# The loads of x of the first three units, issued by ScalarE's queue instead of SyncE's

## The chip, the cores and the metric

The kernel runs on one core of a Trainium2 chip. The metric is the device time of one execution in microseconds; lower is better. TensorE (PE, with its weight loads PEld), VectorE (DVE), ScalarE (ACT) and GpSimd (POOL) compute. SyncE (SP) computes nothing here: it only issues DMAs. ACT can issue DMAs too. All DMAs are carried by the core's 16 DMA engines.

## The reference

Two layers follow each other: a gated linear recurrence over time, and a highway feed-forward layer on its output. There are 4 sequences of 6336 steps with 256 channels, all in float32.

```python
sig = 1.0 / (1.0 + np.exp(-f_logit))
f = lower_bound + (1.0 - lower_bound) * sig
i = 1.0 - f
for t in range(S):
    h = f[:, t] * h + i[:, t] * x[:, t]
    y[:, t] = h
...
H = np.maximum(y @ w_h, 0.0)
T = 1.0 / (1.0 + np.exp(-(y @ w_t + b_t)))
out = T * H + (1.0 - T) * y
```

## The kernel before

The 25344 rows (sequences times steps) are cut into 21 units, numbered 0 to 20. A unit holds blocks of 128 rows: units 0 and 1 have 2 blocks, unit 2 has 4, units 3 to 6 have 8, the middle ones twice 8, the last ones fewer again. So a load of f_logit or of x moves 256 KiB for units 0 and 1, 512 KiB for unit 2 and 1 MiB for units 3 to 6. I call the load of f_logit of unit n "l" with its number (l0), and that of x likewise (x0).

What happens to a unit, with the letters that the kernel's table uses:

- l, x: the two loads (line 250, both through the function load, both on SP's queue)
- u: ACT takes sigmoid(-f_logit) (line 262)
- b: POOL or DVE multiplies u with x; the product is called bv (line 277)
- i, p: PE transposes u and bv so that time runs along the free axis (lines 286, 311)
- f: ACT or DVE makes the gate from the transposed u (lines 301, 299), in two halves of 128 channels
- s: DVE scans along time (line 320), again by halves of the channels; the result is y
- z, g: PE multiplies y with the weights w_t and w_h (lines 333, 145); t, d, e: ACT, DVE and POOL make the gated part (lines 356, 363, 377)
- o, c, w: PE transposes back and adds, ACT or DVE copies, SP stores (lines 393, 394, 405, 403, 411)

The order of all this is written out by hand: a long table of tokens such as `x1.0:1` (load x of unit 1, part 0, into buffer 1), which a loop at the end of the kernel turns into instructions, one after the other. `pin` keeps every instruction in that order on its engine. Tokens `k*4` are filler matmuls on zeros for PE. Each engine works in its own order, and an instruction that waits holds up all behind it.

At the start there are four things besides the units:

- `warm` (line 154): one small sigmoid on ACT, ahead of which the compiler puts ACT's table load
- `prm`: two loads of 1 KiB each, lower_bound and b_t, on ACT's queue (lines 167, 168); PE transposes them (token `pc`, line 209), and DVE makes from that the scales ncc, cc, bt and the diagonals (tokens `cc`, `dg`)
- `wt`, `wh`: the loads of the two weight matrices, 256 KiB each, on SP's queue (lines 202, 205)
- `WT`, `WH`: DVE scales the weights with cc (lines 224 and 230, 232); WT stands between the gates and the first scan's second half of unit 0, WH behind that scan

Waits for loads go by eight counters (DMAHW0 to DMAHW7 in the listings below), which are dealt out to the DMAs in the order of the program, round and round. A DMA may be issued only when the one eight places before it, which has the same counter, has landed. Before the change the order is: first prm load 0, l0 1, x0 2, l1 3, second prm load 4, l2 5, wt 6, x1 7, wh 0, x2 1, l3 2, x3 3, l4 4, x4 5, l5 6.

Of the kernel before, what the change touches and what calls it, by code (L numbers as in the profile page):

```python
# [14 lines left out]
AF = mybir.ActivationFunctionType  # L15
# [4 lines left out]
def kernel(  # L20
# [22 lines left out]
    units, at = [], 0  # L43
# [3 lines left out]
    assert at == B * S  # L47

    order = """
l0.0:0 u0.0:0 pc:0 k*4:1 x0.0:0 b0.0.0v:0 p0.0.0:1 i0.0.1:2 cc dg f0.1v:0 p0.0.1:0 i0.0.0:3 l1.0:1 u1.0:1 l2.0:2  # L50
u2.0:2 s0.1:0 f0.0v:0 i1.0.1:4 i1.0.0:5 k*16:6 wt WT f1.0:1 i2.0.0:0 s0.0:1 z0.0.1:1 x1.0:1 b1.0.0:1 p1.0.1:2 p1.0.0:3
wh WH z0.0.0:5 k*4:6 f1.1:2 i2.0.1:4 g0.0.1:6 f2.0:3 x2.0:2 t0.0.0:0 s1.1:2 g0.0.0:0 l3.0:3 s1.0:3 g1.0.1:2 z1.0.1:3
g1.0.0:5 z1.0.0:7 t0.0.1 B2.0:2 p2.0.1:1 f2.1:0 x3.0:3 p2.0.0:4 d0.0.1:0 e0.0.1 d0.0.0 d1.0.0:1 d1.0.1 k*4:0 u3.0:3
k*4:0 t1.0.1:1 e0.0.0 i3.0.1:0 i3.0.0:2 t1.0.0 e1.0.0 l4.0:4 f3.1:2 s2.1:4 s2.0:5 B3.0v:0 f3.0:1 k*4:1 e1.0.1 x4.0:4
g2.0.0:1 d2.0.0:2 z2.0.0:0 t2.0.0:2 g2.0.1:3 k*1:2 o0.0.0:2 p3.0.1:0 l5.0:0 u4.0:0 z2.0.1:4 t2.0.1 e2.0.0 x5.0:0
# [95 lines left out]

    warm = sb([P, 64], FP32, "warm")
    nc.gpsimd.memset(warm, 0.0)
    nc.scalar.activation(warm, warm, AF.Sigmoid)
# [12 lines left out]
    nc.scalar.dma_start(prm[:NH], lower_bound.rearrange("(h p) -> h p", p=P))
    nc.scalar.dma_start(prm[NH:], moe_b_t.rearrange("(h p) -> h p", p=P))
# [74 lines left out]
    def rows(full, at, j0, j1):  # L243
        return full[at + j0 * P:at + j1 * P, :].rearrange("(p j) d -> p j d", p=P)

    def load(n, s, name, src, slot):
        at, subs = units[n]
        t = sb([P, NB, D], FP32, name, slot)
        j0 = sum(subs[:s])
        pin(nc.sync.dma_start(t[:, :subs[s]], rows(src, at, j0, j0 + subs[s])))  # L250
# [201 lines left out]
```

## Time and profile before

| what | value |
|---|---|
| median of 3 runs | 208.8 us (208.2 to 209.44) |
| the profiled execution's own time | 208.83 us |
| its span, first to last instruction | 207.1 us |
| mean granted TensorE clock | 1.000 |
| moved by the DMA engines | 78.67 MB, 380 GB/s on average |
| reads, writes of HBM | 52.43 MB, 25.95 MB |

The profile comes from one execution. A row of its timeline gives the start in us from the span's start, the time it took in us, the engine, the line of the kernel, the operation, out<-in, the shapes and the count of merged instructions; in brackets stands the idle time of the engine before it and what ended that. ACTq and SPq are the parts of ACT and SP that issue DMAs. The busy shares count instructions that compute; the slices cut the span into 40 equal stretches of 5.2 us. In the page's list of DMA queues, q1 is SP's and q10 is ACT's.

### The profile page before, as it was taken

The page shows a single profiled execution, that of the slowest core. Times are in us where ns is not written, and L with a number is a line of the kernel's source. Part 1 is how long each engine was busy: PE and PEld are TensorE (multiplying, and loading weights), DVE is VectorE, ACT ScalarE, POOL GpSimd, SP SyncE. Part 2 cuts the span into 40 slices and gives each one's busy share as a digit, 9 for nine tenths or more (in the row PEclk, how much of TensorE's full clock was granted, in tenths as well). Part 3 has the DMA queues.
Part 4 walks back from the last instruction along what each step waited for, and adds up shares of the span by engine and source line. Part 5 has one row for each costly group of instructions (what it writes and reads, how often), then busy time and mean ns, then how long its engine had stood idle before and what let it go on. Part 6 is the DMA issues. An engine that isn't in the chain of part 4 may idle for free.

```text
span 207.1 us, 4606 instructions
## 1 busy us (share of the span) xinstructions
PE 194.7 (94%) x1850; PEld 135.0 (65%) x1850; DVE 192.8 (93%) x141; ACT 190.9 (92%) x173; POOL 171.9 (83%) x90
## 2 busy tenths in 40 slices
PE   7999988998799999999989999999999999999991
PEld 2566657556566858747846967658767587677780
DVE  2799989999999999999999979999999999999971
ACT  4479699999999999999998999999999999998792
POOL 3173798978999999978998899979979949999920
PEclk9999999999999999999999999999999999999999
DMA  6999999999999999999999999999999999934576
GB/s 178 365 425 416 418 423 418 418 419 412 425 418 420 420 419 421 424 417 419 427 415 418 423 414 429 418 417 427 412 424 390 403 325 352 364 141 161 206 304 253
DMA packets 15980, 78.67 MB, mean 380 GB/s; under 512 B 1748, under 2 KB 2264, under 8 KB 10072
## 3 DMA queue, kind: packets, MB, share of 16 engines
q1 hardware_dynamic: 15952, 78.39, 93.5%
q8 instruction: 14, 0.23, 0.5%
q14 instruction: 6, 0.05, 0.1%
q10 hardware_dynamic: 8, 0.00, 0.0%
HBM read 52.43 MB, written 25.95 MB: 379 GB/s over the span
## 4 chain that ended last, share of the span: by engine, by line
PE 48%; DVE 17%; ACT 16%; DMA 11%; issue 4%; POOL 2%; SPq 1%; DVEq 0%; ACTq 0%
PE psum L333 13%; PE psum L145 11%; DMA l<-in_f_logit_dram 11%; DVE y L320 10%; PE psum L393 6%; DVE d L363 6%; PE psum L394 6%; ACT f L301 6%; PE psum L286 6%; PE psum L311 5%; ACT u L262 4%; ACT t L356 3%; ACT o L405 2%; POOL bv L277 2%; DVE f L299 1%
## 5 line engine op out<-in xcount | busy, mean ns | idle before, releaser
L277 POOL TENSOR_TENSOR bv<-u,x 128x1024 bf16<-128x1024 f16 (+2 forms) x44 | 99.8, 2293 | 18.3 <-ACT f L301 7.4
L320 DVE TENSOR_TENSOR_SCAN y<-f,y,psum 128x1024 bf16<-128x1024 f16 (+6 forms) x40 | 103.7, 2614 | 1.0 <-ACT f L301 0.6
L377 POOL TENSOR_TENSOR d<-d,t 128x1024 bf16<-128x1024 bf16 (+3 forms) x35 | 71.7, 2063 | 11.4 <-ACT t L356 6.1
L333 PE MATMUL psum<-y,w_sb 128*128 128x512 bf16 (+1 forms) x224 | 77.4, 367 | 3.0 <-ACT f L301 1.9
L145 PE MATMUL psum<-y,w_sb 128*128 128x512 bf16 x184 | 69.7, 379 | 0.7 <-DVE y L320 0.7
L363 DVE SCALAR_TENSOR_TENSOR d<-y,ncc,psum 128x1024 bf16<-128x1024 bf16 (+2 forms) x56 | 62.6, 1147 | 3.4 <-PE psum L145 1.5
L356 ACT ACTIVATE t<-psum,bt 128x1024 bf16<-128x1024 f32 (+2 forms) x56 | 56.3, 1038 | 2.6 <-PE psum L145 1.7
L262 ACT ACTIVATE u<-l 128x2048 f16<-128x2048 f32 (+2 forms) x28 | 48.6, 1747 | 5.4 <-DMA l<-in_f_logit_dram 5.4
L301 ACT ACTIVATE f<-psum,ncc 128x1024 f16<-128x1024 f16 (+3 forms) x38 | 50.9, 1365 | 1.6 <-PE psum L286 1.6
L405 ACT COPY o<-psum 128x1024 f32<-128x1024 f32 (+1 forms) x49 | 48.5, 1031 | 2.2 <-PE psum L394 1.0
L393 PE MATMUL psum<-diag,y 128*128 128x128 f16 x396 | 48.8, 219 | 0.6 <-ACT f L301 0.4
L394 PE MATMUL psum<-ident_b,d 128*128 128x128 bf16 x396 | 48.6, 219 | 0.8 <-DVE d L377 0.8
L394 PEld LDWEIGHTS <-d 128*128 128x128 bf16 x396 | 44.0, 113 | 4.8 <-DVE d L377 1.2
L393 PEld LDWEIGHTS <-y 128*128 128x128 bf16 x396 | 44.2, 113 | 2.5
L333 PEld LDWEIGHTS <-w_sb 128*128 128x128 f16 x224 | 21.6, 98 | 18.1 <-issue 1.0
L145 PEld LDWEIGHTS <-w_sb 128*128 128x128 f16 x184 | 17.9, 97 | 21.3 <-issue 6.0
L311 PE MATMUL psum<-ident_f,bv 128*128 128x128 f32 x198 | 29.3, 276 | 1.3 <-POOL bv L277 0.8
L286 PE MATMUL psum<-ident_h,u 128*128 128x128 f16 x396 | 28.6, 219 | 1.2 <-ACT u L262 0.8
L286 PEld LDWEIGHTS <-u 128*128 128x128 f16 x396 | 25.0, 98 | 6.9 <-ACT u L262 2.1
L311 PEld LDWEIGHTS psum<-ident_f,bv 128*128 128x128 f32 x198 | 22.4, 141 | 7.1 <-POOL bv L277 2.1
L377 DVE TENSOR_TENSOR d<-d,t 128x1024 bf16<-128x1024 bf16 (+3 forms) x15 | 10.6, 718 | 0.2
L145 PE MATMUL psum<-zeros 128*128 128x512 bf16 x39 | 10.6, 399 | 0.0
(33 smaller groups left out, 38.6 us busy)
## 6 DMA issues: line engine op xcount, KB each, us to landing
out_dram<-o SPq DMA_DIRECT2D x48, 512.0 KB, 7.9
l<-in_f_logit_dram SPq DMA_DIRECT2D x23, 1024.0 KB, 14.6
x<-in_x_dram SPq DMA_DIRECT2D x23, 1024.0 KB, 14.4
l<-in_f_logit_dram SPq DMA_DIRECT2D x2, 512.0 KB, 5.9
x<-in_x_dram SPq DMA_DIRECT2D x2, 512.0 KB, 7.4
l<-in_f_logit_dram SPq DMA_DIRECT2D x3, 256.0 KB, 3.7
x<-in_x_dram SPq DMA_DIRECT2D x3, 256.0 KB, 5.5
out_dram<-o SPq DMA_DIRECT2D x3, 256.0 KB, 5.6
```

The costliest lines, as they stand in the source:

```text
L145: return pe.add_instruction(mybir.InstMatmult(name=nc.get_next_instruction_name(), start_tensor_calc=start, stop_tensor_calc=stop, tile_si ...
L277: shared(pin(e.tensor_mul(st[n]["bv", s][:, a:c].rearrange("p k d j -> p k j d"), st[n]["u", s][:, 2 * a:2 * c].rearrange("p (k j) d -> p ...
L286: pin(nc.tensor.transpose(uT[:, j * P:(j + 1) * P], st[n]["u", s][:, j, h * P:(h + 1) * P], ident_h))
L301: pin(nc.scalar.activation(to, of, AF.Identity, scale=ncc[:, h:h + 1], bias=1.0))
L311: pin(nc.tensor.transpose(words[:, k:k + g * (P - 1) + 1:g], pair, ident_f))
L320: pin(nc.vector.tensor_tensor_scan(y[:, c:e], st[n]["f", h][:, c:e], data, 0.0 if fresh else carry[h], op0=ALU.mult, op1=ALU.add))
L333: pin(nc.tensor.matmul(p.part(a, e), w, data, start=ki == 0, stop=ki == NH - 1))
L356: pin(nc.scalar.activation(half(n, q, "t", m), z, AF.Sigmoid, bias=bt[:, m:m + 1]))
L363: pin(nc.vector.scalar_tensor_tensor(half(n, q, "d", m), y, ncc[:, m:m + 1], g, op0=ALU.mult, op1=ALU.max))
L377: shared(pin(e.tensor_mul(d, d, t)), not eng)
L393: pin(nc.tensor.matmul(o, st[n]["y", h][:, whole], diag[:, h], start=True, stop=False))
L394: pin(nc.tensor.matmul(o, half(n, q, "d", h)[:, cols], ident_b, start=False, stop=True))
```

## The change

Three tokens, x0, x1 and x2, leave the table. In their place, ahead of the loop over the table, ACT issues these three loads, with the two prm loads behind the first, and the small sigmoid `warm` follows behind all five.

```diff
-l0.0:0 u0.0:0 pc:0 k*4:1 x0.0:0 b0.0.0v:0 p0.0.0:1 i0.0.1:2 cc dg f0.1v:0 p0.0.1:0 i0.0.0:3 l1.0:1 u1.0:1 l2.0:2
+l0.0:0 u0.0:0 pc:0 k*4:1 b0.0.0v:0 p0.0.0:1 i0.0.1:2 cc dg f0.1v:0 p0.0.1:0 i0.0.0:3 l1.0:1 u1.0:1 l2.0:2
...
-    nc.scalar.activation(warm, warm, AF.Sigmoid)
...
-    nc.scalar.dma_start(prm[:NH], lower_bound.rearrange("(h p) -> h p", p=P))
-    nc.scalar.dma_start(prm[NH:], moe_b_t.rearrange("(h p) -> h p", p=P))
...
-    def load(n, s, name, src, slot):
+    def load(n, s, name, src, slot, queue=nc.sync):
...
-        pin(nc.sync.dma_start(t[:, :subs[s]], rows(src, at, j0, j0 + subs[s])))
+        pin(queue.dma_start(t[:, :subs[s]], rows(src, at, j0, j0 + subs[s])))
...
+    ahead = "x0.0:0 x1.0:1 x2.0:2"
+    for k, token in enumerate(ahead.split()):
+        name, _, slot = token.partition(":")
+        n, s = [int(c) for c in name[1:].split(".")]
+        load(n, s, name[0], xs if name[0] == "x" else logits, slot, nc.scalar)
+        if k == 0:
+            pin(nc.scalar.dma_start(prm[:NH], lower_bound.rearrange("(h p) -> h p", p=P)))
+            pin(nc.scalar.dma_start(prm[NH:], moe_b_t.rearrange("(h p) -> h p", p=P)))
+    pin(nc.scalar.activation(warm, warm, AF.Sigmoid))
```

On SP, at the start of the program, these rows stood before the change (l_98 is l0, x_107 x0, l_126 l1, l_130 l2, x_171 x1, x_198 x2, l_206 l3; the brackets name the counters that a row waits for):

```order
L250 DMA l_98<-in_f_logit_dram 128x512
L250 DMA x_107<-in_x_dram 128x512
L250 DMA l_126<-in_f_logit_dram 128x512
L250 DMA l_130<-in_f_logit_dram 128x1024
L202 DMA w_raw_94<-in_moe_w_t_dram 128x2x256
L250 DMA x_171<-in_x_dram 128x512
L205 DMA w_raw_94<-in_moe_w_h_dram 128x2x256 [waits DMAHW0_49]
L250 DMA x_198<-in_x_dram 128x1024 [waits DMAHW1_49]
L250 DMA l_206<-in_f_logit_dram 128x2048 [waits DMAHW2_49]
```

Now SP has these rows at the same place (l_104 is l0, l_130 l1, l_134 l2, l_206 l3, x_225 x3, l_267 l4, x_284 x4, l_309 l5; the lines moved up by three):

```order
L247 DMA l_104<-in_f_logit_dram 128x512
L247 DMA l_130<-in_f_logit_dram 128x512
L247 DMA l_134<-in_f_logit_dram 128x1024
L199 DMA w_raw_91<-in_moe_w_t_dram 128x2x256 [waits DMAHW0_49]
L202 DMA w_raw_91<-in_moe_w_h_dram 128x2x256 [waits DMAHW1_49]
L247 DMA l_206<-in_f_logit_dram 128x2048 [waits DMAHW2_49]
L247 DMA x_225<-in_x_dram 128x2048 [waits DMAHW3_49]
L247 DMA l_267<-in_f_logit_dram 128x2048 [waits DMAHW4_49]
L247 DMA x_284<-in_x_dram 128x2048 [waits DMAHW5_49]
L247 DMA l_309<-in_f_logit_dram 128x2048 [waits DMAHW6_49,Activation_49]
```

The three loads of x are gone from SP, wt and wh moved up to places four and five, and the counters are dealt anew: x0 0, l0 1, first prm load 2, l1 3, second prm load 4, l2 5, x1 6, x2 7, wt 0, wh 1, l3 2. So wt now waits for x0's landing, wh for l0's and l5 for x1's.

On ACT, at the start of the program, these rows stood before (u_100, u_128 and u_132 are u of units 0, 1 and 2):

```order
L167 DMA prm_88<-in_lower_bound_dram 2x128
L154 ACT_TABLE_LOAD
L154 ACTIVATE warm_63<-warm_63 128x64 [waits Pool_49]
L168 DMA prm_88<-in_moe_b_t_dram 2x128
L262 ACTIVATE u_100<-l_98 128x512 [waits DMAHW1_49]
L262 ACTIVATE u_128<-l_126 128x512 [waits DMAHW3_49]
L262 ACTIVATE u_132<-l_130 128x1024 [waits DMAHW5_49]
```

Now ACT has these (x_95, x_99 and x_101 are x0, x1 and x2; u_106, u_132 and u_136 are u of units 0, 1 and 2):

```order
L247 DMA x_95<-in_x_dram 128x512
L416 DMA prm_87<-in_lower_bound_dram 2x128
L417 DMA prm_87<-in_moe_b_t_dram 2x128
L247 DMA x_99<-in_x_dram 128x512
L247 DMA x_101<-in_x_dram 128x1024
L418 ACT_TABLE_LOAD
L418 ACTIVATE warm_63<-warm_63 128x64 [waits Pool_49]
L259 ACTIVATE u_106<-l_104 128x512 [waits DMAHW1_49]
L259 ACTIVATE u_132<-l_130 128x512 [waits DMAHW3_49]
L259 ACTIVATE u_136<-l_134 128x1024 [waits DMAHW5_49]
```

Five DMAs stand ahead of the table load and of the first sigmoid, where one stood before. The order on PE, DVE and POOL is the same as before.

More of the change, by code (lines that the diff above doesn't have):

```diff
@@ L49 @@
     order = """
-l0.0:0 u0.0:0 pc:0 k*4:1 x0.0:0 b0.0.0v:0 p0.0.0:1 i0.0.1:2 cc dg f0.1v:0 p0.0.1:0 i0.0.0:3 l1.0:1 u1.0:1 l2.0:2
-u2.0:2 s0.1:0 f0.0v:0 i1.0.1:4 i1.0.0:5 k*16:6 wt WT f1.0:1 i2.0.0:0 s0.0:1 z0.0.1:1 x1.0:1 b1.0.0:1 p1.0.1:2 p1.0.0:3
-wh WH z0.0.0:5 k*4:6 f1.1:2 i2.0.1:4 g0.0.1:6 f2.0:3 x2.0:2 t0.0.0:0 s1.1:2 g0.0.0:0 l3.0:3 s1.0:3 g1.0.1:2 z1.0.1:3
+l0.0:0 u0.0:0 pc:0 k*4:1 b0.0.0v:0 p0.0.0:1 i0.0.1:2 cc dg f0.1v:0 p0.0.1:0 i0.0.0:3 l1.0:1 u1.0:1 l2.0:2
+u2.0:2 s0.1:0 f0.0v:0 i1.0.1:4 i1.0.0:5 k*16:6 wt WT f1.0:1 i2.0.0:0 s0.0:1 z0.0.1:1 b1.0.0:1 p1.0.1:2 p1.0.0:3
+wh WH z0.0.0:5 k*4:6 f1.1:2 i2.0.1:4 g0.0.1:6 f2.0:3 t0.0.0:0 s1.1:2 g0.0.0:0 l3.0:3 s1.0:3 g1.0.1:2 z1.0.1:3
 g1.0.0:5 z1.0.0:7 t0.0.1 B2.0:2 p2.0.1:1 f2.1:0 x3.0:3 p2.0.0:4 d0.0.1:0 e0.0.1 d0.0.0 d1.0.0:1 d1.0.1 k*4:0 u3.0:3
```

## The prediction

> **What bounds the kernel now.** I read the page first: the busy shares and the slices of the DMA.
>
> ```profile
> PE 194.7 (94%) x1850; PEld 135.0 (65%) x1850; DVE 192.8 (93%) x141; ACT 190.9 (92%) x173; POOL 171.9 (83%) x90
> GB/s 178 365 425 416 418 423 418 418 419 412 425 418 420 420 419 421 424 417 419 427 415 418 423 414 429 418 417 427 412 424 390 403 325 352 364 141 161 206 304 253
> ```
>
> PE, DVE and ACT are busy 92 to 94% each, so none of them has room for work that comes late. The DMA moves about 420 GB/s from the third slice on; its first slice (5.2 us) has 178. The chain that ended last, in order of time, has two long transfers, of 22 us together:
>
> ```profile
> 2.11 5.94 DMA l<-in_f_logit_dram
> ...
> 8.85 16.13 DMA l<-in_f_logit_dram
> ```
>
> Both are at the start: l2 until 8.05 and l5 until 25. Behind that no transfer stands among its longest pieces. The kernel is therefore bound by loads until 25 us and by three full engines behind that. Windows show how full:
>
> ```profile
> 0.00:5.00 5.00, 3.81 (x10) 1.31 (x11) 1.08 (x5) 2.17 (x3) 1.61 (x11) 1.00 0.70 178
> 5.00:10.00 5.00, 5.00 (x30) 2.57 (x29) 3.76 (x12) 2.41 (x4) 0.36 (x1) 1.00 0.93 353
> 10.00:15.00 5.00, 4.72 (x39) 3.28 (x38) 4.71 (x12) 3.24 (x5) 4.20 (x4) 1.00 1.02 424
> 40.00:60.00 20.00, 17.33 (x166) 11.95 (x165) 19.83 (x13) 19.89 (x16) 17.90 (x8) 1.00 1.01 419
> ```
>
> Behind the stretch and its length stand the busy times of PE, PEld, DVE, ACT and POOL, last the GB/s. From 40 to 60 DVE is busy 19.83 of 20 us and ACT 19.89. A delay that both still have there reaches the end. The change is all in the first 5 us, so what matters is how much of it is left at 25 to 30 us. Next I read the timeline of DVE, since it is the fullest engine there:
>
> ```profile
> 4.20 0.73 DVE L277 TENSOR_TENSOR bv<-u,x 128x512 bf16<-128x512 f16 x1 [3.06 <-ACT u L262]
> 7.65 0.48 DVE L299 TENSOR_SCALAR f<-psum,ncc 128x256 f16<-128x256 f16 x1
> 8.80 0.62 DVE L224 TENSOR_SCALAR w_sb<-w_raw,cc 128x256 f16<-128x256 f32 x2 [0.66 <-DMA w_raw<-in_moe_w_t_dram]
> 9.33 0.68 DVE L320 TENSOR_TENSOR_SCAN y<-f,psum 128x256 bf16<-128x256 f16 x1
> 10.22 0.72 DVE L230 SCALAR_TENSOR_TENSOR w_sb<-w_raw,cc,ndiag 128x128 f16<-128x128 f32 x1 [0.21 <-DMA w_raw<-in_moe_w_h_dram]
> ...
> 16.95 2.72 DVE L277 TENSOR_TENSOR bv<-u,x 128x2048 bf16<-128x2048 f16 x1
> 20.56 4.58 DVE L320 TENSOR_TENSOR_SCAN y<-f,y,psum 128x1024 bf16<-128x1024 f16 x2 [0.26 <-PE psum L311]
> 28.19 2.35 DVE L320 TENSOR_TENSOR_SCAN y<-f,y,psum 128x1024 bf16<-128x1024 f16 x1 [0.62 <-ACT f L301]
> ...
> 35.08 1.28 DVE L363 SCALAR_TENSOR_TENSOR d<-y,ncc,psum 128x1024 bf16<-128x1024 bf16 x1 [0.36 <-PE psum L145]
> ```
>
> DVE waits for the two weight matrices, 0.66 us for w_t (landed just before 8.80) and 0.21 us for w_h (10.2). From 10.22 to 28.2 it has only two idle stretches of note, 0.26 and 0.62 us. So **the two weight loads start the chain of DVE**, and whatever delays them moves it, less 0.9 us at most.
>
> **The change part by part.** *SP's queue.* Three loads leave it, so l1 and l2 are issued about 0.45 us sooner; the DMA engines still work on l0 then. w_t now waits for x0's landing, w_h for l0's. Both then are issued at some 4 us, and six loads of 2 MiB are still queued, so the DMA has work. The later loads (l5 waits for x1's counter in place of w_t's) have long cover: l5 was issued at 8.85 and moved only at about 23 to 25.
>
> *The order of the data.* This is the term that counts. In the old single queue w_t was fifth, behind l0, x0, l1 and l2. Now SP's queue has l0, l1, l2 ahead of it, and ACT's has x0, x1, x2, of the same 1 MiB. If the DMA engines take turns between the two queues, both MiB are through at the same moment, and w_t and w_h come after all six. The same eight transfers were done when these rows say:
>
> ```profile
> 9.53 0.33 SPq L250 DMA_DIRECT2D x<-in_x_dram  x1
> 10.26 0.33 SPq L250 DMA_DIRECT2D l<-in_f_logit_dram  x1
> 11.53 0.33 SPq L250 DMA_DIRECT2D x<-in_x_dram  x1
> ```
>
> Each of these issues waits for the counter of an older load: x1, w_h and x2, landed at about 9.5, 10.2 and 11.5. The bytes are the same, so I take the same total, 11.5, for all eight, and w_h is now the last: 11.5. w_t is before it by one 256 KiB share, 10.26 - 9.53 = 0.73: 10.75. So w_t lands 1.95 us later.
>
> The Trainium skill, "DMA: Bandwidth & Descriptors", section "Issuing engines are not separate DMA queues", says that loads from several engines run on the same 16 DMA engines and that a second issuer saves only issue time. By it the total stays at 11.5, as I take it; by its opposite see the second rival.
>
> *DVE.* w_t's product goes from 8.80 to 10.76. The scan behind it ran from 9.33 to 10.01, so it ends at 11.97; w_h is there at 11.5, and its products start at 11.98 instead of 10.22: **+1.76**. That holds for the product bv of unit 3 as well, because DVE's rows have no idle time between 10.22 and 19.67 (16.95 + 2.72).
>
> *From there to ACT.* PE takes bv of unit 3 from DVE and goes on in its order, through its last matmuls of unit 2, to the transposes of u4, which ACT needs:
>
> ```profile
> 22.48 0.61 PE L286 MATMUL psum<-ident_h,u 128*128 128x128 f16 x8
> 23.18 1.11 ACT L301 ACTIVATE f<-psum,ncc 128x1024 f16<-128x1024 f16 x1 [0.81 <-PE psum L286]
> 25.07 1.91 ACT L262 ACTIVATE u<-l 128x2048 f16<-128x2048 f32 x1 [0.77 <-DMA l<-in_f_logit_dram]
> ```
>
> f4 goes from 23.18 to 24.94 and ends at 26.05; l5 is there as before at 25.0 (the same 7.5 MiB, its own among them, are through by then). u5 starts at about 26.0 instead of 25.07: **+0.93**; the 0.77 us in which ACT waited for l5 are used up. f4's second half and DVE's scan at 28.19 follow ACT: 29.1. DVE's own work before that scan ended at 28.19 - 0.62 = 27.57, and now at 27.57 + 1.76 - 0.26 = 29.07. Both are late by 0.9, and both are full from there: +0.9 at the end.
>
> *ACT's queue.* Five DMA issues now stand ahead of the table load. Before:
>
> ```profile
> 0.73 0.54 ACTq L167 DMA_DIRECT2D prm<-in_lower_bound_dram  x1
> 1.18 0.42 SPq L250 DMA_DIRECT2D x<-in_x_dram  x1
> 1.31 1.28 ACT L154 ACT_TABLE_LOAD   x1 [1.31 <-PEq L436]
> 1.38 0.24 ACTq L168 DMA_DIRECT2D prm<-in_moe_b_t_dram  x1
> 2.60 0.26 ACT L154 ACTIVATE warm<-warm 128x64 f32<-128x64 f32 x1
> 3.06 0.47 SPq L250 DMA_DIRECT2D x<-in_x_dram  x1
> 3.47 0.63 ACT L262 ACTIVATE u<-l 128x512 f16<-128x512 f32 x1 [0.61 <-DMA l<-in_f_logit_dram]
> 3.86 0.26 PE L209 MATMUL psum<-ident_f,prm 4*128 4x4 f32 x1
> ```
>
> A 128-row load takes 0.42 to 0.47 us to issue on SP and is not shown on ACT. By these rows, x0 0.42, two prm 0.24 each, x1 and x2 0.47 each and five gaps of 0.05 end at 2.8; with 1.28 and 0.26 u0 starts at 4.35 instead of 3.47, +0.9. At 0.54 for each, the dearest issue on ACT, it is 5.2, +1.7. Either is hidden: f0's second half would end at 8.13 + 0.9 = 9.0, at most 9.9, and w_t is there at 10.75. If w_t came on time, only the 0.66 us of waiting would cover it.
>
> *The small loads prm.* They now stand behind x0 in ACT's queue, and PE's transpose of prm, first in PE's order but for the six warm-up matmuls, waits for both. How two busy queues share an engine is shown by one event, the data packets of the two prm loads, the only ones on ACT's queue. The first load's stand in the 0.1 us from 1.6, with its counter writes:
>
> ```profile
> q10 hardware_dynamic: 4, 0.00, 4.2%
> ```
>
> The second load's stand in the 0.1 us from 3.1:
>
> ```profile
> q10 hardware_dynamic: 2, 0.00, 3.4%
> ```
>
> The first needed 0.9 to 1.0 us from its issue at 0.73, with nothing else queued. The second was issued at 1.38, so it was ready near 2.3 and waited 0.8 us more, until about the end of l0 (u0 starts on it at 3.47). I read that as turns of a whole load's share. Then, on the two engines that carry prm, its first load follows l1 and its second follows l2:
>
> ```profile
> 5.37 0.63 ACT L262 ACTIVATE u<-l 128x512 f16<-128x512 f32 x1 [1.28 <-DMA l<-in_f_logit_dram]
> 8.08 1.06 ACT L262 ACTIVATE u<-l 128x1024 f16<-128x1024 f32 x1 [2.07 <-DMA l<-in_f_logit_dram]
> ```
>
> l1 landed before 5.37 and l2 before 8.08, on the slowest engine. l2's 512 KiB need 1.24 us at the 424 GB/s of the window from 10, so its share is through between 6.6 and 8.05. At 6.6 the transpose moves by 2.74, and with it what hangs on PE: f0's second half ends at 8.13 + 2.74 = 10.87, 0.1 behind w_t, which I leave out. At 8.1 it is the first rival; with short turns it is nothing. I take 6.6: the later end is that of one engine, the earlier the rate of most rows.
>
> *What comes sooner gains nothing.* x1 and x2 land about 3 and 1.5 us sooner, but unit 1's scans stand behind w_h's products on DVE, and unit 2's behind those.
>
> Sum: the profiled execution took 208.83 us (span 207.1 and 1.7 around it), 0.03 over the median of 208.8. 208.83 + 0.93 = **209.8**, slower by 0.45%.
>
> **The rivals.**
> 1. *prm behind a late l2.* If the engines with prm are among the late ones, prm's transpose comes at 8.1, +4.2. f0's second half ends at 12.4, w_h's products start at 13.6, +3.4, and u5 is late by 3.4 - 0.8 = 2.6: 211.4. For it: PE's row of the transpose stands ahead of all its other work but the warm-up. Against it: l2's 8.05 is the landing of the slowest engine, and the two with prm must be among those.
> 2. *The start gets faster.* In windows of 0 to 5 and 5 to 10 us the DMA moved 0.89 and 1.77 MB; at the 424 GB/s of the next window these need 6.3 us instead of the 8.3 since the first packets at about 1.7. If two queues win all of that, w_t is there at 8.8 and prm early (short turns). DVE then is late only by ACT's queue, 0.9 less the 0.66 and 0.21 of waiting, and ACT need not wait for l5: u5 starts at 24.5, -0.6, DVE at 27.7, -0.45: 208.4. At best all three early waits of DVE (0.26, 0.62 and 0.36) go: 207.7. It decides from the point where w_t lands before 9.1. For it: SP issues almost without a break at the start. Against it is the poorest stretch, 4.25 to 6.5, with over 1 MiB queued (eight loads of 2.5 MiB issued by 4.52, under 0.9 MB moved by 5.0), where more issuers add nothing (the DMA in that stretch, and SP's eighth issue):
>
> ```profile
> DMA packets 249, 0.57 MB, mean 253 GB/s; under 512 B 23, under 2 KB 109, under 8 KB 249
> ```
>
> ```profile
> 4.05 0.47 SPq L250 DMA_DIRECT2D x<-in_x_dram  x1
> ```
>
>    The Trainium skill, "Perfetto Trace Analysis", section "DMA Optimizations", says that spreading issues may help when the issuing engine's track is solid with them; it is, and this rival is what that would give.
> 3. *No effect.* SP's queue is served first while it has work: w_t keeps its time, only x comes later, and the rest hides: 208.8 to 209.0.
>
> **How the numbers follow.** The forecast has 0.52, the rivals 0.22, 0.18 and 0.08. About 0.5% is what a measurement of this kernel can tell from no change, here 1.04 us. The forecast's own range is 209.3 to 210.3 (a queue that starts sooner by up to 0.4, late followers by up to 0.5), so half of it is over the bound: 0.26 slower, 0.26 the same. The first rival is slower (0.22). Of the second, 0.08 is faster and 0.10 the same; the third is the same. Faster 0.08, same 0.44, slower 0.48. From 208.2 to 211.4 about 0.1 is left out on each side.
>
> **What would show it.** In the changed kernel's timeline: five issues on ACT until about 2.8 and u0 at 4.35; prm's transpose at 6.6 (8.1: first rival; under 4.5: short turns); w_t's product at 10.7 and w_h's at 12.0 (8.8 and 10.4: second rival); u5 at 26.0 and DVE's scan at 29.1; the same busy windows behind 40 us. I am wrong if w_t lands before 9.5, or if DVE has lost less than 1 us at w_h's products, or if a delay at 29 us is gone at 60.

## The result, and the profile after

The changed kernel took 209.31 us in the median of 22 runs (208.82 to 210.98), the kernel before 208.56 us (207.71 to 209.5, 22 runs beside them). The ratio is 1.0044, with a 95% interval of 1.0029 to 1.0058: slower by 0.44%. That is under the 0.5% that the prediction gave as the least that can be told from no change, but with this many runs the interval still excludes no change. The profiled execution took 209.57 us (span 207.8) against 208.83 (span 207.1), +0.74. The changed kernel's line numbers are three lower in what follows: 221 and 227 are the weights' products, 317 the scan, 259 u, 206 the transpose of prm.

The page first: busy shares and the slices of the DMA.

```profile
PE 195.0 (94%) x1850; PEld 135.5 (65%) x1850; DVE 193.0 (93%) x141; ACT 190.8 (92%) x173; POOL 172.2 (83%) x90
GB/s 189 387 421 419 418 423 415 419 424 410 419 419 423 419 416 428 423 416 417 427 414 416 402 397 425 423 415 426 415 424 390 396 332 322 372 114 169 205 303 252
```

The busy times are the same within 0.5 us. The DMA moved more in the first two slices (189 and 387 GB/s, before 178 and 365), so the loss does not come from fewer bytes at the start. The windows say the same (stretch, its length, busy PE, PEld, DVE, ACT and POOL, clock, DMA share, GB/s):

```profile
0.00:5.00 5.00, 2.74 (x6) 0.72 (x6) 0.27 (x1) 1.72 (x3) 1.62 (x11) 1.00 0.51 179
5.00:10.00 5.00, 4.54 (x21) 2.63 (x22) 3.52 (x12) 2.98 (x5) 2.21 (x2) 1.00 1.02 387
10.00:15.00 5.00, 5.00 (x37) 3.12 (x36) 4.67 (x10) 2.00 (x4) 1.10 (x1) 1.00 1.02 425
...
40.00:60.00 20.00, 17.54 (x166) 11.97 (x164) 19.80 (x13) 19.89 (x16) 17.93 (x8) 1.00 1.01 418
```

PE was busy 2.74 us in the first five, before 3.81, and ACT 2.00 us from 10 to 15, before 3.24. From 40 to 60 nothing has changed. So the loss is made in the first 15 us. The chain of waits has other early pieces than before, where the two longest were loads of f_logit:

```profile
1.74 3.58 DMA prm<-in_moe_b_t_dram
9.22 3.27 PE psum L145 x15
```

The chain now begins with the second of the two **1 KiB loads of prm** and then runs through PE's **filler matmuls on zeros**. Neither had been in the prediction's sum. DVE's timeline at the start:

```profile
5.48 0.74 DVE L274 TENSOR_TENSOR bv<-u,x 128x512 bf16<-128x512 f16 x1 [4.35 <-ACT u L259]
...
9.36 0.48 DVE L296 TENSOR_SCALAR f<-psum,ncc 128x256 f16<-128x256 f16 x1
9.86 1.64 DVE L221 TENSOR_SCALAR w_sb<-w_raw,cc 128x256 f16<-128x256 f32 x2
11.43 0.67 DVE L317 TENSOR_TENSOR_SCAN y<-f,psum 128x256 bf16<-128x256 f16 x1
12.02 0.32 DVE L227 SCALAR_TENSOR_TENSOR w_sb<-w_raw,cc,ndiag 128x128 f16<-128x128 f32 x1
...
12.72 0.27 DVE L229 TENSOR_SCALAR w_sb<-w_raw,cc 128x128 f16<-128x128 f32 x1
13.15 1.39 DVE L317 TENSOR_TENSOR_SCAN y<-f,y,psum 128x256 bf16<-128x256 f16 x2 [0.15 <-PE psum L308]
...
29.12 2.34 DVE L317 TENSOR_TENSOR_SCAN y<-f,y,psum 128x1024 bf16<-128x1024 f16 x1
```

Three things stand out. The same two products of w_t took 1.64 us instead of 0.62. DVE no longer has a wait for w_t or w_h that shows: it came free at 9.84 (9.36 + 0.48), and w_t landed at that moment. And the scan of unit 1, the row at 13.15 (11.52 before), waited last for PE's transposes of bv (line 308), not for DVE's own work. POOL's rows of the two kernels explain the first; before, then after:

```profile
9.63 1.17 POOL L277 TENSOR_TENSOR bv<-u,x 128x512 bf16<-128x512 f16 x1 [7.40 <-ACT f L301]
11.60 2.15 POOL L277 TENSOR_TENSOR bv<-u,x 128x1024 bf16<-128x1024 f16 x1 [0.80 <-DMA x<-in_x_dram]
```

```profile
7.68 3.41 POOL L274 TENSOR_TENSOR bv<-u,x 128x512 bf16<-128x512 f16 x2 [5.43 <-DMA x<-in_x_dram]
```

x1 and x2 now land so early that POOL runs both products in one piece, until 11.09, right across DVE's products of w_t; before, the first began when w_t's were done and the second when w_h's were. (The bracket at 9.63 names ACT, but x1 had landed only just before 9.53, by the issue of SP that waits for it.) PE's rows of the two kernels explain the third; before, then after:

```profile
3.86 0.26 PE L209 MATMUL psum<-ident_f,prm 4*128 4x4 f32 x1
...
6.52 0.38 PE L239 MATMUL psum<-zeros 128*128 128x512 bf16 x1
6.74 3.40 PE L145 MATMUL psum<-zeros 128*128 128x512 bf16 x15
...
10.86 0.44 PE L311 MATMUL psum<-ident_f,bv 128*128 128x128 f32 x2 [0.28 <-POOL bv L277]
```

```profile
5.46 0.23 PE L206 MATMUL psum<-ident_f,prm 4*128 4x4 f32 x1 [1.53 <-DMA prm<-in_moe_b_t_dram]
...
8.58 0.63 PE L236 MATMUL psum<-zeros 128*128 128x512 bf16 x1
9.01 3.48 PE L145 MATMUL psum<-zeros 128*128 128x512 bf16 x15
...
12.77 0.38 PE L308 MATMUL psum<-ident_f,bv 128*128 128x128 f32 x2
```

From prm's transpose on, PE has no idle time until 12.77. It started 1.60 late, its sixteen fillers (token `k*16`) 2.06 late, and the transposes of unit 1's bv, which stand behind them, 1.91 late. The 0.46 us between prm and the fillers are mostly slower rows of PE (six transposes of u0 in 0.85 us at 7.94, before 0.50 at 6.18); this is seen where PE had first waited over 1 us for prm, at a granted clock shown as 1.00, and why is not shown. Before, PE still had 0.28 us of slack there, waiting for POOL.

ACT and SP, last, give the landings, since an issue of SP waits for the counter of an older load (at 4.99 w_t's issue for x0, at 8.89 for x2, at 9.90 for w_t, at 11.71 for w_h):

```profile
2.89 1.28 ACT L418 ACT_TABLE_LOAD   x1 [2.89 <-issue]
4.18 0.26 ACT L418 ACTIVATE warm<-warm 128x64 f32<-128x64 f32 x1
4.82 1.38 ACT L259 ACTIVATE u<-l 128x512 f16<-128x512 f32 x2 [0.38 <-DMA l<-in_f_logit_dram]
...
24.82 1.11 ACT L298 ACTIVATE f<-psum,ncc 128x1024 f16<-128x1024 f16 x1 [0.69 <-PE psum L283]
25.83 1.90 ACT L259 ACTIVATE u<-l 128x2048 f16<-128x2048 f32 x1
```

```profile
4.99 0.38 SPq L199 DMA_DIRECT2D w_raw<-in_moe_w_t_dram  x1
...
8.89 0.46 SPq L247 DMA_DIRECT2D x<-in_x_dram  x1
9.90 0.33 SPq L247 DMA_DIRECT2D l<-in_f_logit_dram  x1
11.71 0.33 SPq L247 DMA_DIRECT2D x<-in_x_dram  x1
```

l0 and x0, issued on two queues in the same moment (0.74 and 0.73), landed nearly together, at 4.8 and just before 4.99; before, l0 landed alone at 3.47.

### The profile page after: what moved, and what is told of

It is laid out like the page before. It is cut to its first block, busy times and chain, and to the rows that moved or that the text cites. A ratio compares the mean times of both kernels' runs of the same rounds, so it can differ in the third digit from the quotient of the medians.

```text
span 207.8 us, 4606 instructions
## 1 busy us (share of the span) xinstructions
PE 195.0 (94%) x1850; PEld 135.5 (65%) x1850; DVE 193.0 (93%) x141; ACT 190.8 (92%) x173; POOL 172.2 (83%) x90
## 4 chain that ended last, share of the span: by engine, by line
PE 58%; DVE 17%; ACT 14%; issue 5%; POOL 2%; DMA 2%; ACTq 0%; DVEq 0%
PE psum L145 16%; PE psum L330 15%; DVE y L317 10%; PE psum L283 7%; PE psum L390 6%; PE psum L308 6%; PE psum L391 6%; DVE d L360 6%; ACT f L298 6%; ACT t L353 3%; ACT u L259 3%; POOL bv L274 2%; ACT o L402 2%; DMA prm<-in_moe_b_t_dram 2%; PE psum L236 1%
## 5 line engine op out<-in xcount | busy, mean ns | idle before, releaser
L283 PE MATMUL psum<-ident_h,u 128*128 128x128 f16 x396 | 29.1, 221 | 0.5 <-ACT f L298 0.4
L374 DVE TENSOR_TENSOR d<-d,t 128x1024 bf16<-128x1024 bf16 (+3 forms) x15 | 10.4, 708 | 0.2
```

Source lines behind the costliest of these rows:

```text
L283: pin(nc.tensor.transpose(uT[:, j * P:(j + 1) * P], st[n]["u", s][:, j, h * P:(h + 1) * P], ident_h))
L374: shared(pin(e.tensor_mul(d, d, t)), not eng)
```

## The experiments

My first theory was that POOL's early products cost the time, by holding DVE's products of the weights, and that an order or a wait could give it back; the rivals were the late front (u0, x0, prm) and w_t's later landing. Each kernel ran five rounds beside the kernel before. One table first, since the same two numbers decide in all of them. Each trace is one execution, and in three kernels it lies far from the median: b_x1 (210.77 against 209.03), a_warm (209.64 against 210.83) and a_act (208.92 against 209.78); the ratio is that of all runs. "PE" is the start of the transposes of unit 1's bv, "DVE" the start of the last product of w_h; then the start of the scan of unit 1, the start of DVE's scan of unit 4 (28.19 and 29.12 in the rows quoted), the profiled execution, and the ratio to before with its interval.

| kernel | PE | DVE | scan 1 | scan 4 | profiled | ratio |
|---|---|---|---|---|---|---|
| before | 10.86 | 11.33 | 11.52 | 28.19 | 208.83 | 1 |
| after | 12.77 | 12.72 | 13.15 | 29.12 | 209.57 | 1.0044 [1.0029, 1.0058] |
| a_pool | 13.01 | 14.08 | 14.28 | 30.09 | 210.54 | 1.0083 [1.006, 1.0106] |
| a_prm | 14.46 | 14.65 | 14.99 | 31.92 | 212.38 | 1.0163 [1.0131, 1.0196] |
| a_wts | 14.98 | 15.34 | 15.54 | 31.35 | 211.81 | 1.013 [1.0102, 1.0159] |
| b_order | 13.08 | 13.43 | 13.63 | 31.11 | 211.57 | 1.0113 [1.0071, 1.0155] |
| a_pool2 | 12.50 | 12.37 | 12.88 | 28.86 | 209.32 | 1.0048 [1.0023, 1.0074] |
| a_x0 | 12.60 | 13.14 | 13.33 | 29.15 | 209.59 | 1.0063 [1.004, 1.0087] |
| b_x1 | 13.95 | 11.53 | 14.34 | 30.31 | 210.77 | 1.0036 [1.0006, 1.0066] |
| b_wact | 11.13 | 13.48 | 13.68 | 29.50 | 209.98 | 1.0095 [1.0063, 1.0126] |
| a_act | 12.13 | - | 12.51 | 28.48 | 208.92 | 1.0032 [1.0, 1.0064] |
| b_act | 10.40 | - | 10.84 | 27.84 | 208.39 | 0.9983 [0.996, 1.0007] |
| a_warm | 12.86 | 12.99 | 13.24 | 29.21 | 209.64 | 1.0112 [1.0072, 1.0151] |
| a_both | 14.23 | - | 14.61 | 30.59 | 211.02 | 1.0101 [1.0058, 1.0144] |

Three readings. The scan of unit 1 starts 0.38 to 0.53 after the PE number or 0.19 to 0.34 after the DVE number, whichever is later: **two branches meet there**. And profiled time less scan 4 is 180.64 before and 180.43 to 180.55 in all the others: what is lost at 29 us reaches the end in full, but for 0.1 to 0.2 us. From scan 1 to scan 4 it takes 15.81 to 15.98 us in all kernels but four: before (16.67) and b_act (17.00), where scan 4 waits for what follows l5's landing, and a_prm (16.93) and b_order (17.48), where PE's granted clock fell to 0.83. In those two, 1.0 and 1.5 us of the loss come behind scan 1 and not from the two branches.

**a_pool: the changed kernel, POOL's bv of unit 1 waits for w_t's products** (a dependency that the kernel already uses elsewhere).

```diff
-            pin(nc.vector.tensor_scalar(w_sb[:, 1, h], w_raw[:, 1, h], cc[:, h:h + 1], None, op0=ALU.mult))
+            shared(pin(nc.vector.tensor_scalar(w_sb[:, 1, h], w_raw[:, 1, h], cc[:, h:h + 1], None, op0=ALU.mult)), False)
```

> The changed kernel, with one wait more: POOL's first product (bv of unit 1) waits for the end of DVE's w_t products. In the changed kernel POOL ran that product and the next from 7.68 to 11.09, and DVE's first w_t product took 1.38 us instead of some 0.3. Theory (late weights): w_h landed at 11.64, so its products can start at 11.7 at the earliest instead of 12.02; the end comes 0.2 to 0.4 us sooner than in the changed kernel, and over the kernel before remain 0.5 to 0.7 us. Rival (DVE loses its time because POOL works beside it): w_t's products take 0.6, and the whole 1.0 us comes back; within 0.2 us of the kernel before.

Measured: 210.28 us, slower still. w_t's products took 0.61 again, but POOL's two products only moved on to w_h's. Late weights don't explain it: w_h, issued at 5.04, landed 4.9 us later, and its products began at 10.87. Its timelines of POOL and of DVE:

```profile
10.51 3.31 POOL L274 TENSOR_TENSOR bv<-u,x 128x512 bf16<-128x512 f16 x2 [8.26 <-DVE w_sb L221]
```

```profile
9.75 0.61 DVE L221 TENSOR_SCALAR w_sb<-w_raw,cc 128x256 f16<-128x256 f32 x2
...
10.87 0.94 DVE L227 SCALAR_TENSOR_TENSOR w_sb<-w_raw,cc,ndiag 128x128 f16<-128x128 f32 x1
11.74 2.16 DVE L229 TENSOR_SCALAR w_sb<-w_raw,cc 128x128 f16<-128x128 f32 x1
13.82 0.34 DVE L227 SCALAR_TENSOR_TENSOR w_sb<-w_raw,cc,ndiag 128x128 f16<-128x128 f32 x1
```

The hold is shown: a product of 0.27 us lasts 2.16 us and ends just behind POOL (13.82). It is a hold for a whole POOL product, twice in a row here: the first w_h product gets through where bv of unit 1 ends (10.51 + 1.17), the second where bv of unit 2 ends. The Trainium skill, "SBUF — State Buffer", section "SBUF: two separate sides", says just that: GpSimd and certain DVE operations (fast modes that use both port pairs, or two SBUF inputs) share a pair of ports that one of them holds exclusively for a whole instruction. The trace agrees, by 0.94 and 2.16 us here and 1.64 in the changed kernel.

**a_prm: the changed kernel, the two prm loads ahead of x0 on ACT's queue.**

```diff
+    pin(nc.scalar.dma_start(prm[:NH], lower_bound.rearrange("(h p) -> h p", p=P)))
+    pin(nc.scalar.dma_start(prm[NH:], moe_b_t.rearrange("(h p) -> h p", p=P)))
     for k, token in enumerate(ahead.split()):
...
-        if k == 0:
-            pin(nc.scalar.dma_start(prm[:NH], lower_bound.rearrange("(h p) -> h p", p=P)))
-            pin(nc.scalar.dma_start(prm[NH:], moe_b_t.rearrange("(h p) -> h p", p=P)))
```

> The changed kernel, with the two prm loads ahead of x0 on ACT's queue. Theory (late weights): PE's transpose of prm comes near 4 instead of 5.46, but w_t still lands near 9.8 and w_h near 11.6, so the end moves by less than 0.3 us. Rival (ACT's queue delays the front of the program, prm and u0): DVE's second half of f0 ends 1 us sooner than 9.84, w_t's products follow at 8.8 to 9.2 if the weights are there, and 0.5 us or more of the loss goes. If l0 lands near 3.4 again instead of 4.8, then x0's issue beside l0's is what made the first load late.

Measured: 212.16 us, the slowest of all. The front did come back: prm's transpose is at 3.86 and the sixteen fillers end at 10.45 (10.14 before). But w_t landed only at 11.0, although it was issued at 2.14 and not at 4.99; why is open. Its products were held until 13.0 by bv of unit 2 (10.89 to 13.02), and now PE waited for DVE:

```profile
14.08 0.59 PE L330 MATMUL psum<-y,w_sb 128*128 128x256 bf16 x2 [3.41 <-DVE y L317]
```

PE, idle for 3.41 us, then ran at a granted clock of 0.83 in the windows from 10 to 15 and from 15 to 20, so its rows grew (0.59 for 0.38). So prm's place behind x0 is what delayed it, but what an early prm is worth isn't shown here, since the other branch came later. On the last question of the expectation: l0 landed by 3.65 (SP's issue of w_h waits for it), with x0 issued 0.83 us behind it.

**a_wts: the changed kernel, w_t and w_h ahead of l2 on SP.** The tokens `wt wh` move from the table's second and third rows to behind `l1.0:1`; nothing else.

> The changed kernel, with the weight loads moved up on SP's queue: l0, l1, w_t, w_h, l2. Theory (late weights): both weights land before 9, w_h's products start when DVE is free, and at least half of the loss goes (0.4 us or more under the changed kernel). Rival (POOL beside DVE, and prm): w_t's products still start at 9.8 behind f0 and still take 1.6, w_h's at 12.0; no change against the changed kernel beyond 0.2 us.

Measured: 211.23 us. The move dealt the eight counters anew, and x2's issue on ACT had to wait until x0 had landed: the issues of x1 and x2, 0.84 us together in the changed kernel, took 3.15 us here (from 2.02), the table load came at 5.20 and u0 at 6.66. Both weights landed early (w_t, issued at 1.65, 4.5 us later; w_h, at 2.11, 5.4 us later), but w_t's products started only at 11.63, since the front came late, and were held to 14.0. What it shows is that a DMA issue that waits on ACT holds up ACT's computing.

**b_order: the kernel before, all on SP, in the order in which the data of the changed kernel moved** (l0, x0, l1, l2, x1, x2, w_t, w_h).

```diff
-l0.0:0 ... l1.0:1 u1.0:1 l2.0:2
-u2.0:2 ... k*16:6 wt WT f1.0:1 ... x1.0:1 b1.0.0:1 ...
-wh WH ... f2.0:3 x2.0:2 t0.0.0:0
+l0.0:0 ... l1.0:1 u1.0:1 l2.0:2 x1.0:1 x2.0:2
+u2.0:2 ... wt wh k*16:6 WT f1.0:1 ... b1.0.0:1 ...
+WH ... f2.0:3 t0.0.0:0
```

> The kernel before, all on SP's queue as it was, but in the order in which the changed kernel's data moved: l0, x0, l1, l2, x1, x2, w_t, w_h. ACT, prm and the table load are as before. Theory (the order of the data): the loss of the change is there without any second queue, 0.6 to 1.0 us over the kernel before. Rival (ACT's queue delays prm, the table load and u0): no change within 0.3 us of the kernel before, apart from what POOL's earlier product costs DVE.

Measured: 211.02 us, worse than the change. prm was early (3.86), the fillers ended at 10.4, but w_t's products began at 10.27, when w_t landed, and took 1.95 us under POOL's 8.37 to 11.81. With the order alone the DVE branch loses 2.1 us at the scan of unit 1, 0.5 more than with the change; a further 1.5 us come behind that scan, where the granted clock was 0.83. So late weights and an early POOL cost time without any second queue.

**a_pool2: the changed kernel, POOL's bv of unit 1 waits for w_t's products and that of unit 2 for w_h's.** To a_pool's edit comes:

```diff
-            pin(nc.vector.tensor_scalar(w_sb[:, 0, h, rest], w_raw[:, 0, h, rest], cc[:, h:h + 1], None,
-                                               op0=ALU.mult))
+            shared(pin(nc.vector.tensor_scalar(w_sb[:, 0, h, rest], w_raw[:, 0, h, rest], cc[:, h:h + 1], None,
+                                               op0=ALU.mult)), False)
```

> The changed kernel with POOL's two early products put back where the old kernel had them by luck of the landings: bv of unit 1 waits for DVE's w_t products, bv of unit 2 for its w_h products. New theory (DVE's products of the weights stand still while a product on POOL runs): w_t's products take 0.6 us, w_h's are held by one POOL product only (0.4 to 0.9 us) and not by two as in the run with one wait; DVE's first scan of unit 1 starts at 12.4 to 12.7 instead of 13.15, and the end comes 0.4 to 0.7 us sooner than in the changed kernel: 0 to 0.3% over the kernel before. Rival (late weights alone): w_h is there at 10 to 11.6, so the scan still starts near 13 and the time stays within 0.2 us of the changed kernel.

Measured: 209.32 us, ratio 1.0048 against the changed kernel's 1.0044: no gain in the median, 0.25 us in the profiled execution. The hold shrank to 0.6 us (the first product of w_h, 0.94 at 11.04), DVE was ready at 12.63, and waited 0.25 us for PE. This is where the first theory falls: POOL's hold is real, but another branch is as late.

**a_x0: the changed kernel with only x0 (and prm behind it) on ACT; x1 and x2 back on SP.**

```diff
-    ahead = "x0.0:0 x1.0:1 x2.0:2"
+    ahead = "x0.0:0"
```

(with x1 and x2 back in the table, where they stood before)

> Part of the change alone: only x0 on ACT's queue, ahead of the prm loads and the table load; x1 and x2 go back to SP, behind w_t and w_h as before. Theory (x1 and x2 early on POOL, and the weights behind them, make the loss): w_t lands near 8.5, x1 near 9.2, and only the front is late (l0 at 4.4 to 4.8, f0 until 9.8): w_t's products start at 9.8, +1.0, w_h's at 10.9 to 11.6, and the kernel is slower than before by 0 to 0.4 us. Rival (the front makes the loss): 0.7 to 1.0 us, as with the whole change.

Measured: 209.73 us, ratio 1.0063. Moving x0 alone costs as much as the whole change: prm's transpose at 5.25, PE's branch at 12.60; POOL's bv of unit 2 (10.47 to 12.61) held the first product of w_h, which took 2.08 us. DVE's rows:

```profile
9.15 0.48 DVE L296 TENSOR_SCALAR f<-psum,ncc 128x256 f16<-128x256 f16 x1
9.56 0.61 DVE L221 TENSOR_SCALAR w_sb<-w_raw,cc 128x256 f16<-128x256 f32 x2
...
10.68 2.08 DVE L227 SCALAR_TENSOR_TENSOR w_sb<-w_raw,cc,ndiag 128x128 f16<-128x128 f32 x1
```

Neither weight was late here: w_t, issued at 2.11, landed 5.3 us later, and w_h, issued at 4.73, 4.1 us later. w_t's products still start at 9.56, right behind the gate f0, which waits for PE and prm. The late front alone makes DVE's products late.

**b_x1: the kernel before with only x1 on ACT's queue, behind prm.**

```diff
+    load(1, 0, "x", xs, "1", nc.scalar)
```

(`x1.0:1` leaves the table)

> The other part, the smallest of it: only x1 on ACT's queue, behind the prm loads and beside the table load, so that the front stays as it was. New theory (POOL beside DVE): x1 lands near 5 to 6, POOL's product of unit 1 runs from about 6 to 7.3, ahead of w_t's products (8.8) and out of the way of w_h's (0.9 us in place of 1.3): no loss, 0 to 0.4 us faster than before. Rival (a second queue beside SP's delays the loads of f_logit and the weights): l2 and w_t land 0.7 us later and the kernel loses 0.2 to 0.5 us.

Measured: 209.03 us (208.17 to 211.92), ratio 1.0036. prm was early (3.97), no product of DVE was held, and yet the scan of unit 1 was the latest but three, because l1 landed late (7.64 by the landings in the trace, 5.35 before), PE's fillers behind u1's transposes began at 8.75, and its clock fell to 0.80 and 0.86 in the windows from 5 and from 10. PE's and DVE's rows:

```profile
9.18 4.50 PE L145 MATMUL psum<-zeros 128*128 128x512 bf16 x15
```

```profile
14.34 1.39 DVE L320 TENSOR_TENSOR_SCAN y<-f,y,psum 128x256 bf16<-128x256 f16 x2 [2.53 <-PE psum L311]
```

DVE waits 2.53 us for PE behind its fillers: the PE branch by itself. This execution took 210.77 us, 1.7 over the median, so it shows the branch and not what the median execution loses.

**b_wact: the kernel before with both weight loads on ACT's queue, behind prm.** The two `dma_start` of w_t and w_h are issued by `nc.scalar` ahead of the table.

> The kernel before with the two weight loads on ACT's queue behind the prm loads, and x as before on SP. Theory (w_t and w_h start DVE's chain): both land by 7 to 8, w_t's products follow f0 at 8.1 and w_h's at 9.3; l2 lands up to 1.4 us later. DVE's chain starts 0.3 to 0.9 us sooner, of which l5's landing (25.0) lets through 0 to 0.4: same to 0.4 us faster than before. Rival (l2, not the weights, starts the chain): l2 late by 1.4, the scans of units 1 and 2 late with it, 0.5 us or more slower.

Measured: 210.33 us. w_t's products started at 8.18, 0.6 earlier than before, but w_h landed at 10.7, and POOL's products of units 1 and 2 (9.91 to 13.22) held one product of w_h for 2.16 us. PE's branch was at 11.13: the DVE branch by itself.

After these eight the theory was changed to: the weights' products are held by POOL, and ACT could do them, if POOL does not hold ACT's operations too.

**a_act and b_act: the weights' plain scaling on ACT instead of DVE**, in the changed kernel and in the one before. DVE keeps the two diagonal blocks of w_h.

```diff
-            pin(nc.vector.tensor_scalar(w_sb[:, 1, h], w_raw[:, 1, h], cc[:, h:h + 1], None, op0=ALU.mult))
+            pin(nc.scalar.activation(w_sb[:, 1, h], w_raw[:, 1, h], AF.Identity, scale=cc[:, h:h + 1]))
...
-            pin(nc.vector.tensor_scalar(w_sb[:, 0, h, rest], w_raw[:, 0, h, rest], cc[:, h:h + 1], None,
-                                               op0=ALU.mult))
+            pin(nc.scalar.activation(w_sb[:, 0, h, rest], w_raw[:, 0, h, rest], AF.Identity, scale=cc[:, h:h + 1]))
```

(`f1.0:1 f1.1:2` stand together at WT, ahead of it in a_act, behind it in b_act)

> The changed kernel, but w_t's scaling and the two blocks of w_h that need only a factor are done by ACT instead of DVE (with unit 1's two gates ahead of them on ACT); DVE keeps w_h's two diagonal blocks. Theory (DVE's products of the weights stand still while a POOL product runs; ACT's do not): ACT scales w_t at 9.8 to 10.6 with no row over 0.5 us although POOL runs bv of units 1 and 2 until about 11.1; DVE's second scan of unit 0 starts at about 9.9 instead of 11.43; unit 1's scan starts at 11.9 to 12.6 instead of 13.15; DVE's scan of unit 4 at 28.2 to 28.7 instead of 29.12; total 208.5 to 209.1, ratio to before 0.999 to 1.002. Rival (the 1.38 us were the weights' slow arrival or the form of the product, not POOL): a scaling row on ACT takes over 1 us too, unit 1's scan starts at 13 or later, total 209.3 to 209.8.

Measured: profiled 208.92, scan of unit 4 at 28.48, as expected; but the median of 12 runs is 209.78 (207.95 to 210.08), over the expected 209.1, and the ratio 1.0032 [1.0, 1.0064] leaves open whether it beats the change. ACT, POOL, DVE and PE in turn:

```profile
9.34 0.91 ACT L221 ACTIVATE w_sb<-w_raw,cc 128x256 f16<-128x256 f32 x2
```

```profile
7.39 3.39 POOL L273 TENSOR_TENSOR bv<-u,x 128x512 bf16<-128x512 f16 x2 [5.15 <-DMA x<-in_x_dram]
```

```profile
10.17 1.02 DVE L227 SCALAR_TENSOR_TENSOR w_sb<-w_raw,cc,ndiag 128x128 f16<-128x128 f32 x2
12.51 1.39 DVE L316 TENSOR_TENSOR_SCAN y<-f,y,psum 128x256 bf16<-128x256 f16 x2 [1.32 <-PE psum L307]
```

```profile
8.45 3.40 PE L145 MATMUL psum<-zeros 128*128 128x512 bf16 x15
```

The two rows on ACT take 0.91 us together with POOL running all along (7.39 to 10.78): nothing holds ACT. DVE is free at 11.2, and then **waits 1.32 us for PE**, whose fillers run until 11.85. With the hold out of the way, PE's branch stands alone, and the scan of unit 1 is still 1.0 us later than before. This execution is 0.65 us faster than the changed kernel's. The end of the hold alone could have given no more than 0.15 us, DVE's wait for PE in the changed kernel; the rest needed PE to be sooner too: prm's transpose came 0.31 earlier (5.15), and the sixteen fillers took 0.3 less (8.23 to 11.85, against 8.58 to 12.49).

> The kernel before with the same move of the weights' scaling to ACT. Theory: DVE saves its wait for w_t and two rows, its first diagonal block at 10.2 is still held by POOL until 10.8; unit 1's scan starts at about 11.3 instead of 11.52, but ACT's u5 waits for l5 at 25.0 as before, so DVE's scan of unit 4 stays within 0.3 us of 28.19: total 208.3 to 208.7, ratio 0.998 to 1.001. Rival (DVE's early work alone bounds the start): unit 4's scan is earlier by the 0.6 us that DVE gives away and the total is 208.0 or less.

Measured: 208.12 us, ratio 0.9983 [0.996, 1.0007]: 0.2 us under the expected times, and no difference that can be told from none. The scan of unit 1 is 0.68 earlier, that of unit 4 0.35. The second waits for ACT's gate, and ACT's u5, which waits for l5, also began 0.35 earlier (24.72 for 25.07), so the 0.35 are l5's landing in this execution and not shown to come from the edit:

```profile
27.84 2.35 DVE L319 TENSOR_TENSOR_SCAN y<-f,y,psum 128x1024 bf16<-128x1024 f16 x1 [0.73 <-ACT f L300]
```

It has the lowest median of the kernels run here, but it is not shown to beat the kernel before.

**a_warm: the changed kernel with the small sigmoid ahead of ACT's five issues. a_both: that and a_act's edit.**

```diff
+    pin(nc.scalar.activation(warm, warm, AF.Sigmoid))
     ahead = "x0.0:0 x1.0:1 x2.0:2"
...
-    pin(nc.scalar.activation(warm, warm, AF.Sigmoid))
```

> The changed kernel with the small sigmoid, and so its table load, ahead of the five issues on ACT again: l0 then starts alone on its queue and x0 is issued at about 2.9. Theory (l0 was late because x0 was issued in the same moment on the other queue): u0 starts at 3.4 to 3.7 instead of 4.82, x0 lands at 5.0 to 5.5 and bv of unit 0 starts about 5.3 (5.48 in the changed kernel), prm's transpose is at 6.0 or later instead of 5.46; x1 and x2 land later than 7.5 and 8.8, so POOL's two products end later than 11.1 and w_h's products are held; total 209.0 to 210.0. Rival (l0 is late whenever a second queue has work before it has landed): u0 at 4.3 or later again.

> Both edits together: the weights scaled on ACT, the small sigmoid first. Theory: no row of ACT's scaling is over 0.5 us, w_h's diagonal blocks on DVE can still be held by POOL until about 12; unit 1's scan at 12.0 to 13.0, DVE's scan of unit 4 at 28.2 to 28.9, total 208.5 to 209.3. Rival (POOL is not the cause): no gain over the kernel with the small sigmoid first alone.

Measured: 210.83 and 210.87 us. The test of u0 failed, by a side effect: the counters were dealt anew, x2's issue had to wait for l1's landing (5.18 by the landings in the trace), and ACT with it (ACT's issues of x1 and x2 in one row, x2's own from 5.2, then SP's, of a_warm; w_h's issue at 3.93 waits for l0's counter):

```profile
2.19 3.36 ACTq L247 DMA_DIRECT2D x<-in_x_dram  x2
```

```profile
3.93 0.38 SPq L202 DMA_DIRECT2D w_raw<-in_moe_w_h_dram  x1
```

u0 came at 5.61, though l0 had landed by 3.93. That landing bears on the question all the same: x0 was issued at 0.92 here, 0.18 behind l0, and l0 landed 0.9 earlier than in the changed kernel, where both were issued at once. So the rival (late whenever a second queue has work) doesn't hold, and in the two kernels with this lead (a_both has l0 by 3.98) it was enough to take most of the delay away. In a_both prm's transpose came at 7.09 and PE's branch at 14.23, so its two edits tell nothing together: it was slower than a_act, and no faster than a_warm in the median.

## Why the prediction was right, and where it was not

The forecast of 209.8 in all, +0.97 on the profiled execution's 208.83, stands against +0.74 between the profiled executions and +0.75 between the medians; the sign, the place and the size of the delay at 29 us are right, with 209.31 at the lower edge of the range of 209.3 to 210.3. The way there is right only from 12 us on, and that the sum before it came out is luck, as the next points show.

- **What bounds the kernel.** Right. All of the delay at DVE's scan of unit 4 (+0.93) reaches the end, less 0.2, and in fourteen kernels what follows that scan takes the same within 0.21 us.
- **SP's queue.** w_t was issued at 4.99 and not at some 4; x0 was late. What that cost is not shown; in a_prm w_t was issued at 2.14 and landed later still.
- **The order of the data.** The total of the eight loads is right in this execution: 11.5 was predicted, and w_h had landed at 11.71. In a_pool, a_pool2 and a_act, which issue these loads in the same order, w_h landed at 10.0 to 10.1 and w_t at 9.3, under the 9.5 that the prediction had named as a sign of being wrong. The term "w_t lands 1.95 us later" is too large: it landed before 9.86, 1.06 later. And it is not "the term that counts". f0's second half, behind prm and PE, started 1.71 late (9.36 for 7.65); less the 0.66 us that DVE had waited for w_t before, that alone makes w_t's products about 1.06 late. With w_t there sooner they still started 0.40 to 0.41 behind the start of that gate, in a_pool (9.75), a_pool2 (9.93) and a_x0 (9.56); in the changed kernel it is 0.50, so w_t's landing cost at most 0.1.
- **DVE.** w_t's products were to start at 10.76 and started at 9.86; w_h's were to start at 11.98 and started at 12.02. The sum is right by two errors that cancel, which is luck: w_t's products started 0.9 sooner than predicted, and took 1.02 longer (1.64 for 0.62), because POOL held them.
- **"What comes sooner gains nothing."** This step failed. x1 and x2 did land sooner, and it cost: POOL ran bv of both units across w_t's products. The old table had its loads of x1 and x2 so late that POOL began each product where DVE had just finished with the weights (9.63 behind w_t's, 11.60 behind w_h's).
- **The small loads prm.** The time was to be 6.6 and was 5.46, about 0.5 behind x0: neither turns of a whole l2 nor short ones. The larger error is in what follows: "with it what hangs on PE: f0's second half ends at ... 10.87, 0.1 behind w_t, which I leave out". The step followed PE's delay only into the gate f0 and left it there, as hidden behind w_t; but f0 came as late as w_t (9.84). Behind the gate's transposes PE has sixteen fillers in its fixed order, 3.6 to 3.9 us in which it can't catch up, and behind them the transposes of unit 1's bv. The 1.60 us of prm went through all of it and made the scan of unit 1 wait for PE: the changed kernel's chain of waits says so, a_pool2 and a_act confirm it from the other side, by taking DVE out of the way. With prm at 6.6 this branch alone would have been about 1.1 later than it was (an estimate from 6.6 - 5.46).
- **ACT's queue.** The five issues ended at 2.86 (2.8 predicted); u0 came at 4.82 and not at 4.35, as l0 landed late, which the prediction didn't have. It cost nothing further, since PE reached u0's transposes only behind prm.
- **From there to ACT and the end.** Right: u5 at 25.83 (26.0 predicted), without waiting for l5, and DVE's scan at 29.12 (29.1).
- **The rivals.** A start that gets faster: the DMA did move more by 10 us, 2.83 MB (179 and 387 GB/s for 5 us each) against 2.66, but as x and not as l0 and prm. In a_pool, a_pool2 and a_act, where the eight loads were through by about 10.1, a faster start gained nothing either, as the scan of unit 1 waited for PE or for the hold. The others didn't occur.

So the cause is two branches of nearly one length, both made later by the change, and both at first by prm behind x0: PE's through prm and the fillers (scan of unit 1 at 13.15), and DVE's through the gate f0, with w_t landing at the same moment, and POOL's hold (ready at 13.0). Shown: prm's delay by x0 (a_prm, a_x0), the hold (a_pool, b_wact), PE's branch by itself (b_x1, a_act), and that taking away only the hold gives little or nothing (a_pool2, a_act). Not shown: a version of the changed kernel with both repaired; a_both was to come near and failed at its front. Not run: x1 and x2 on ACT behind prm with x0 left on SP, which would part x0's share from theirs. Also open is why l2 landed later in the kernel before (u2, which waits for it, began at 8.08) than in the changed one (7.12); in b_act, with the loads of the kernel before, u2 began at 7.27, so executions differ by that much.

## What to carry to other kernels

When a load is moved, follow every engine's fixed order to the next place where two engines meet, filler work included: a 1 KiB load that an in-order engine waits for first can cost more than 1 MiB that nobody waits for. A transfer that lands early also starts its consumer early, and the consumer may then run beside something that it holds; ask not only who is late but what will now run at the same time. Before a wait is shortened on one branch, read how late the other branch is: here DVE's slack of 0.15 us against PE left the end of a hold of 1.02 us nearly without effect.

## What the runs showed of the hardware that was not expected

- In the first 15 us of these traces DVE's products from SBUF to SBUF stand still until a running POOL product ends: 0.27 us became 2.16 (a_pool), 0.32 became 2.08 (a_x0), 0.25 became 1.14 (a_wts). DVE's scans and gates, which read PSUM, were not held (0.69 at 9.57 in a_act, with POOL at work from 7.39 to 10.78), nor were ACT's.
- Two loads of 256 KiB issued in the same moment on two queues landed together late: l0 at 4.8 instead of 3.47 (4.57 in a_x0, by 4.43 in a_pool). A lead of 0.18 us brought l0 back to 3.9. A load of 1 KiB in the same moment on the other queue did no harm: prm's, at 0.73 in the kernel before, with l0 at 3.47.
- A DMA issue that waits for a counter on ACT's queue holds ACT's computing: u0 at 5.61 (a_warm), 5.67 (a_both) and 6.66 (a_wts). Moving one instruction in the program's order was enough to deal the eight counters so.
- PE's granted clock fell to 0.80 to 0.86 over some 10 us when PE had been idle for 2.27 to 3.41 us near the start (a_prm, b_order, b_x1). But in a_both PE was idle for 3.16 us, until 7.09, and the granted clock stayed at 1.00, so idle time alone is not shown to be the cause.
